# Attention scores: split float32r products of one head, or plain float32 products of two heads in the two row halves of the array

## The chip, the cores and the metric

The kernel runs on one NeuronCore of a Trainium2 chip. Its engines are TensorE (PE in the profile, with its weight loads on a row of their own, PEld), VectorE (DVE), ScalarE (ACT), GpSimd (POOL) and SyncE (SP), which in this kernel issues every DMA. The metric is the device time of one execution in microseconds (us), and lower is better. All inputs lie in device memory when the time begins.

## The reference, cut to what matters

The inputs are q, k, v of 4 batches x 12 heads x 448 tokens x 64 features. Attention with normalised queries and keys is followed by two feed-forward blocks on the 1792 x 768 features.

```python
def rmsnorm(x, g):
    return x / np.sqrt(np.mean(x * x, axis=-1, keepdims=True) + 1e-06) * g
q_n, k_n = rmsnorm(q, g_q), rmsnorm(k, g_k)
scores = q_n @ k_n.T / sqrt(64)                     # per head: 448 x 448
attn = exp(scores - max(scores)); attn = attn / (sum(attn) + 1e-09)
x = attn @ v                                        # heads side by side: 1792 x 768
h = x @ w_in;  x = max(0.01 * h, h) @ w_out         # 768 -> 2048 -> 768
out = ((x @ w1) * (x @ w2)) @ w3 @ w_last           # 768 -> 1024 -> 1024 -> 768
```

## The kernel before, in words

There are 48 heads, taken one by one in slots `s = 0..47`. The 448 query rows of a head are four chunks of 112. In the slot of a head, `scores(s, c)` (L272) makes for each chunk a 112 x 448 tile of scores in PSUM, VectorE scales it, takes the row minimum of the negated scores and writes it to SBUF (`p<-ps`, L289), and ScalarE makes the exponential with its row sum (`p<-p`, L298). One slot later `p_transpose` (L320) turns the four 112 x 448 tiles of a head on TensorE (`pt`, L327, 16 transposes a head), and the results go to SBUF by turns on VectorE and ScalarE (`pth`). Two slots after its scores, every second head, `values` (L349) multiplies the transposed tiles of a pair of heads with v: plain float32 products, 64 columns wide, the two heads in the two column halves of the array, by turns, into one bank (`po`, L121). The helper `together` (L113) keeps these matmuls next to each other.

The products of the feed-forward part, and of the scores, are split: a float32 operand x is rounded to float32r (`xh`), the rest x - xh is a second one (`xl`), and products of the parts are summed in PSUM. For the scores of a head the keys' two parts stand on top of each other in the 128 rows (`ks`: kh in rows 0 to 63, kl in rows 64 to 127), and the queries are there twice (`qt` is loaded into both halves): one matmul with `qh` (L285) and one with `ql` (L286) give all four partial products. `qh` is a copy on ScalarE, `ql` a subtraction on GpSimd (`prep`, L215). The keys of a pair are loaded (`kt_sb`, L255), scaled with the norms on VectorE (L260), rounded on ScalarE (`kh`, L262), subtracted on VectorE (L264), and four DMAs put the parts into `ks` (L268, L269), since the halves of a tile sit in other rows there.

The feed-forward work is one stream of matmul groups (`ps_mm`, L527; three matmuls for each 128 x 128 weight block: wh with xh, wh with xl, wl with xh). `fill` (L1011) puts it between the steps of attention in even shares: first the product of w3 and w_last (`pw`, slots 5 to 17), then the first two batches. Weights arrive as 64-bit words and pass through GpSimd, ScalarE and VectorE before use (`w`, `raw`, `wh`, `wl`; L431 to L488). A planner that simulates the program sets the order of the instructions on each engine, by the priorities in `PRIORITY`; on the chip each engine, SP included, keeps that order. When attention is done (about 800 us), the last two batches run without it (`ps_a`, `ps_b`, `ps_c`, `ps_o`).

```python
ps_sc = right(name="ps_sc", bufs=2, space=PSUM)                                  # L89
nc.tensor.matmul(ps, h["qh"][:, q], h["ks"], start=True, stop=False)             # L285
nc.tensor.matmul(ps, h["ql"][:, q], h["ks"], start=False, stop=True)             # L286
```

Of the kernel before, what the change touches and what calls it, by code (L numbers as in the profile page):

```python
# [8 lines left out]
F32 = mybir.dt.float32  # L9
# [29 lines left out]
MAX_GROUP = 8  # L39
TOGETHER = 2000  # L40
# [8 lines left out]
def attention_then_moe(  # L49
# [39 lines left out]
    ps_sc = right(name="ps_sc", bufs=2, space=PSUM)  # L89
# [97 lines left out]
    def load(i):  # L187
        if i >= NH:
            return
        h = heads[i]  # L190
        b, j = divmod(i, H)
        if i < 2:
            h["k"] = io.tile([CP, NCH, D], F32, tag="rb", name="k_sb", bufs=2)
            nc.sync.dma_start(h["k"], qk[b, j, :, 1])
        h["qt"] = io.tile([P, S], F32, tag="qt", name="qt_sb")
        nc.sync.dma_start(h["qt"][0:D], qt[b, j])
        dma = nc.sync.dma_start(h["qt"][D:P], qt[b, j])
        if i == 2:
            start["ins"] = dma

    def load_v(i):

        if i % 2 or i >= NH:
            return
        b, j = divmod(i, H)
        x = io.tile([CP, 2, NCH, D], F32, tag="v", name="v_sb", bufs=3)
# [17 lines left out]
    def first_keys(i):  # L224

        h = heads[i]
        kn = att.tile([CP, NCH, 2, D], F32, tag="qh", name="kn", bufs=2)
        for e in range(2):
            nc.gpsimd.tensor_tensor(
                kn[:, :, e], h["k"], h["rk"].unsqueeze(2).to_broadcast([CP, NCH, D]), op=ALU.mult  # L230
            )
# [7 lines left out]
        if i == 0:  # L239
            pair = att.tile([P, 2, S], F32R, tag="ks", name="ks", bufs=2)  # L240
            for e in range(2):
                heads[e]["ks"] = pair[:, e]
        ks = h["ks"].rearrange("q (p c) -> q p c", c=NCH)
        pk = pk[:, :S].rearrange("q (c p) -> q p c", c=NCH)
        start["keys"] = nc.scalar.activation(ks, pk, AF.Copy, scale=gqk)
        nc.vector.scalar_tensor_tensor(
            ks[D:P], pk[D:P], gqk[D:P], ks[D:P].bitcast(F32), op0=ALU.mult, op1=ALU.subtract
        )

    def keys(i):  # L250
# [3 lines left out]
        k = io.tile([P, S], F32, tag="kt", name="kt_sb", bufs=1)  # L254
# [10 lines left out]
        pair = att.tile([P, 2, S], F32R, tag="ks", name="ks", bufs=2)  # L265
        for e in range(2):
            rows = slice(e * D, (e + 1) * D)
            nc.sync.dma_start(pair[0:D, e].bitcast(F32), kh[rows].bitcast(F32))  # L268
            nc.sync.dma_start(pair[D:P, e].bitcast(F32), kl[rows].bitcast(F32))  # L269
            heads[i + e]["ks"] = pair[:, e]  # L270

    def scores(i, c):  # L272
        if i >= NH:
            return
        h = heads[i]
        if c == 0:
            h["p"] = [None] * NCH
            if i % 2 == 0:
                sums = small.tile([CP, 2, NCH], F32, tag="sum", name="sum")
                for e in range(2):  # L280
                    heads[i + e]["sum"] = sums[:, e]
                heads[i + 1]["sums"] = sums
# [827 lines left out]
```

## Time and profile before

| what | value |
|---|---|
| time, median of 3 runs | 1256.22 us (1252.75 to 1260.56) |
| the profiled execution, its own time | 1252.88 us |
| its span in the profile | 1251.1 us |
| TensorE busy, mean granted clock | 1151.0 us (92%), 0.962 |
| VectorE / ScalarE / GpSimd busy | 769.4 / 661.4 / 226.5 us |
| moved by DMA | 191.44 MB, 51.0% of the 16 engines' span |

A busy time counts the moments in which an instruction of an engine was under way; matmuls overlap in it, since one begins before the results of the last are written. The granted clock is 1.0 at 2.4 GHz and 0.5 at 1.2 GHz. "A <- B" in a view of waits says that A stood idle until B was done.

### The profile page before, as it was taken

What the parts mean: (1) busy time and instruction counts of PE and PEld (TensorE: products, weight loads), DVE (VectorE), ACT (ScalarE), POOL (GpSimd) and SP (SyncE); (2) the same over time, 40 slices, a digit from 0 to 9 for tenths busy, and PEclk for the clock granted to TensorE, in tenths of its full rate; (3) what the DMA queues carried; (4) which work ended last, traced back from release to release, by engine and by line L of the source; (5) the groups of instructions that cost most, each with busy time, mean ns of one, the idle gap of its engine ahead of it and who ended that gap; (6) DMA issues with size and microseconds to landing.
All of it is one profiled execution on the core that took longest, in us unless ns stands there. A gap on an engine that the chain in (4) does not pass through costs nothing.

```text
span 1251.1 us, 16792 instructions
## 1 busy us (share of the span) xinstructions
PE 1151.0 (92%) x5816; PEld 976.7 (78%) x5816; DVE 769.4 (61%) x1449; ACT 661.4 (53%) x1308; POOL 226.5 (18%) x211
## 2 busy tenths in 40 slices
PE   3659898999888999898999999999999999899998
PEld 1438686876566888686888888899999999799997
DVE  6788776779755466663785355267346465954553
ACT  5766766677656556454765465245442434533431
POOL 4232222334212123213542211100000000000000
PEclk9769999888998999998999999999999999899999
DMA  7777768989889975564464243153212121212212
GB/s 226 195 203 214 215 189 269 292 284 290 251 245 273 240 202 162 151 187 137 148 218 130 79 133 134 53 167 110 81 34 76 35 76 42 73 38 73 63 35 97
DMA packets 105221, 191.44 MB, mean 153 GB/s; under 512 B 22992, under 2 KB 61872, under 8 KB 105136
## 3 DMA queue, kind: packets, MB, share of 16 engines
q1 hardware_dynamic: 105136, 190.37, 51.0%
q8 instruction: 45, 0.74, 0.3%
q14 instruction: 40, 0.33, 0.1%
HBM read 136.74 MB, written 43.03 MB: 144 GB/s over the span
## 4 chain that ended last, share of the span: by engine, by line
PE 54%; DMA 14%; DVE 7%; ACT 4%; issue 3%; SPq 2%; POOL 1%; ACTq 0%; DVEq 0%; POOLq 0%
PE ps_mm L527 19%; PE ps_o L527 13%; PE ps_b L527 9%; PE ps_c L527 5%; DMA w<-w_in 3%; DMA w<-w_out 3%; PE ps_a L527 2%; PE pt L327 2%; PE po L121 2%; DMA ks<-kt_sb 2%; DMA kt_sb<-kt 1%; DMA wh<-kept_first_mlp_h 1%; PE ps L285 1%; DVE raw L460 1%; PE ps L286 1%
## 5 line engine op out<-in xcount | busy, mean ns | idle before, releaser
L213 DVE TENSOR_TENSOR wl<-raw,wh 128x512 fp32r<-128x512 f32 (+1 forms) x136 | 112.6, 831 | 73.0 <-ACT wh L485 37.8
L527 PE MATMUL ps_mm<-xh,wh 128*128 128x448 f32 x384 | 146.6, 383 | 10.6 <-DMA wh<-kept_first_mlp_h 6.9
L327 PE MATMUL pt<-ident,p 112*112 112x112 f32 x768 | 115.3, 276 | 42.2 <-ACT pth L101 21.3
L327 PEld LDWEIGHTS pt<-ident,p 112*112 112x112 f32 x768 | 88.1, 141 | 77.2 <-ACT pth L101 27.6
L289 DVE TENSOR_SCALAR_CACHE_REDUCE p<-ps,rs 112x448 f32<-112x448 f32 x192 | 126.1, 676 | 33.8 <-PE ps L286 20.4
L527 PE MATMUL ps_mm<-xh,wl 128*128 128x448 f32 x384 | 145.5, 379 | 1.5 <-DMA wl<-kept_first_mlp_l 1.5
L298 ACT ACTIVATE p<-p,low 112x448 f32<-112x448 f32 x192 | 127.2, 663 | 36.1 <-DVE p L289 35.7
L527 PE MATMUL ps_mm<-xl,wh 128*128 128x448 f32 x384 | 145.1, 378 | 0.0
L451 ACT ACTIVATE w<-w 128x768 uint32<-128x768 uint32 (+1 forms) x80 | 63.7, 797 | 109.3 <-DMA w<-w_in 36.2
L456 DVE SCALAR_TENSOR_TENSOR raw<-w,raw 128x768 uint32<-128x768 uint32 (+1 forms) x80 | 71.4, 892 | 79.9 <-ACT w L454 79.6
L449 POOL TENSOR_SCALAR raw<-w 128x768 f32<-128x768 f32 (+1 forms) x80 | 70.0, 875 | 265.8 <-DVE wl L213 99.5
L527 PE MATMUL ps_mm<-gh,wh 128*128 128x448 f32 x288 | 106.7, 372 | 2.7 <-DMA wh<-kept_first_mlp_h 1.3
L527 PE MATMUL ps_mm<-gh,wl 128*128 128x448 f32 x288 | 105.7, 369 | 0.0
L527 PE MATMUL ps_mm<-gl,wh 128*128 128x448 f32 x288 | 105.4, 367 | 0.0
L527 PE MATMUL ps_o<-gl,wh 128*128 128x448 f32 x288 | 104.7, 365 | 0.0
L527 PE MATMUL ps_o<-gh,wl 128*128 128x448 f32 x288 | 102.5, 365 | 0.0
L527 PE MATMUL ps_o<-gh,wh 128*128 128x448 f32 x288 | 99.4, 366 | 0.8 <-DVE s L940 0.8
L285 PE MATMUL ps<-ks,qh 128*112 128x448 f32 x192 | 80.2, 422 | 16.4 <-DMA ks<-kt_sb 6.7
L527 PEld LDWEIGHTS ps_mm<-xh,wh 128*128 128x128 f32 x384 | 75.1, 196 | 19.9 <-DMA wh<-kept_first_mlp_h 7.4
L213 POOL TENSOR_TENSOR gl<-y,gh 128x448 fp32r<-128x448 f32 x48 | 58.9, 1229 | 161.6 <-ACT gh L101 154.9
L527 PEld LDWEIGHTS ps_mm<-xh,wl 128*128 128x128 f32 x384 | 75.0, 195 | 10.5 <-issue 2.1
L213 POOL TENSOR_TENSOR ql<-qt_sb,qh 128x448 fp32r<-128x448 f32 x48 | 61.1, 1273 | 114.2 <-ACT qh L101 71.0
(129 smaller groups left out, 2556.1 us busy)
## 6 DMA issues: line engine op xcount, KB each, us to landing
w<-w_in SPq DMA_DIRECT2D x16, 768.0 KB, 7.4
w<-w_out SPq DMA_DIRECT2D x24, 512.0 KB, 5.2
w<-w SPq DMA_DIRECT2D x16, 768.0 KB, 4.9
qk_sb<-qk SPq DMA_DIRECT2D x48, 224.0 KB, 4.9
qt_sb<-qt SPq DMA_DIRECT2D x96, 112.0 KB, 4.0
w<-w3t SPq DMA_DIRECT2D x16, 512.0 KB, 4.6
w<-w_last SPq DMA_DIRECT2D x8, 768.0 KB, 6.2
kept_first_mlp<-raw SPq DMA_DIRECT2D x16, 384.0 KB, 4.0
```

The lines of the kernel that those rows point to most:

```text
L121: one = nc.tensor.matmul(out, a, x, start=begin, stop=end)
L213: e.tensor_tensor(out, x, y.bitcast(F32), op=ALU.subtract)
L285: nc.tensor.matmul(ps, h["qh"][:, q], h["ks"], start=True, stop=False)
L286: nc.tensor.matmul(ps, h["ql"][:, q], h["ks"], start=False, stop=True)
L289: nc.vector.tensor_scalar(p, ps, h["scale"][:, c : c + 1], None, op0=ALU.mult, op1=ALU.min, accum_out=low,)
L298: exps[i] = nc.scalar.activation(p, p, AF.Exp, bias=low, scale=-1.0, accum_out=h["sum"][:, c : c + 1])
L327: nc.tensor.transpose(pt[:, c * CP : (c + 1) * CP], h["p"][c][:, kc * CP : (kc + 1) * CP], ident[:CP, :CP],)
L449: nc.gpsimd.tensor_scalar(out, h, 0.0, 1.0, op0=ALU.mult, op1=ALU.mult)
L451: nc.scalar.activation(low, low, AF.Copy, scale=2.0**-29)
L456: nc.vector.scalar_tensor_tensor(top, high, 3, top, op0=ALU.logical_shift_left, op1=ALU.bitwise_or)
L460: nc.vector.tensor_tensor(top, top, low, op=ALU.add)
L527: nc.tensor.matmul(ps[:, :n], a, x, start=begin, stop=end, skip_group_check=on)
```

## The change

The scores become plain float32 products: the keys of a pair stay as they are after scaling (`kt_sb`, rows 0 to 63 of one head, 64 to 127 of the other), the queries of a pair are loaded once into one tile in the same layout, and a step makes the scores of one chunk for both heads with two matmuls of 64 rows each, one in each half of the array's rows, into the two banks of one PSUM tile. `prep`, the rounding and subtraction of the keys and the four `ks` DMAs are gone. There is one PSUM tile of two banks in place of two tiles of one; `kt` and `qt` have three buffers (one and two before), `p` has twelve in place of seven. Transposes come two slots after the scores and `values` three, since the scores of a pair take two slots, two chunks of both heads in each.

```diff
+PBUFS = 12
...
-    ps_sc = right(name="ps_sc", bufs=2, space=PSUM)
+    ps_sc = right(name="ps_sc", bufs=1, space=PSUM)
...
     def load(i):
-        if i >= NH:
+        if i % 2 or i >= NH:
             return
...
-        h["qt"] = io.tile([P, S], F32, tag="qt", name="qt_sb")
-        nc.sync.dma_start(h["qt"][0:D], qt[b, j])
-        dma = nc.sync.dma_start(h["qt"][D:P], qt[b, j])
+        h["qt"] = io.tile([P, S], F32, tag="qt", name="qt_sb", bufs=3)
+        dma = nc.sync.dma_start(h["qt"], qt[b, j : j + 2].rearrange("h d s -> (h d) s"))
...
-    def prep(i):
-        if i >= NH:
-            return
-        h = heads[i]
-        h["qh"] = att.tile([P, S], F32R, tag="qh", name="qh", bufs=2)
-        copy("A", h["qh"], h["qt"])
-        h["ql"] = att.tile([P, S], F32R, tag="ql", name="ql", bufs=2)
-        subtract("P", h["ql"], h["qt"], h["qh"])
...
     def keys(i):
...
-        k = io.tile([P, S], F32, tag="kt", name="kt_sb", bufs=1)
+        k = io.tile([P, S], F32, tag="kt", name="kt_sb", bufs=3)
...
         nc.vector.scalar_tensor_tensor(k, k, gqk, rk, op0=ALU.mult, op1=ALU.mult)
-        kh = att.tile([P, S], F32R, tag="kh", name="kh", bufs=1)
-        copy("A", kh, k)
-        kl = k.bitcast(F32R)
-        subtract("V", kl, k, kh)
-        pair = att.tile([P, 2, S], F32R, tag="ks", name="ks", bufs=2)
-        for e in range(2):
-            rows = slice(e * D, (e + 1) * D)
-            nc.sync.dma_start(pair[0:D, e].bitcast(F32), kh[rows].bitcast(F32))
-            nc.sync.dma_start(pair[D:P, e].bitcast(F32), kl[rows].bitcast(F32))
-            heads[i + e]["ks"] = pair[:, e]
+        heads[i]["k"] = k
 
     def scores(i, c):
...
-        ps = ps_sc.tile([P, 512], F32, tag="sc", name="ps")[:CP, :S]
         q = slice(c * CP, (c + 1) * CP)
-        nc.tensor.matmul(ps, h["qh"][:, q], h["ks"], start=True, stop=False)
-        nc.tensor.matmul(ps, h["ql"][:, q], h["ks"], start=False, stop=True)
-        p = h["p"][c] = att.tile([CP, S], F32, tag="p", name="p", bufs=7)
...
+        ps = ps_sc.tile([P, 2, 512], F32, tag="sc", name="ps")[:CP, :, :S]
+        one = pair[0]
+        together((ps[:, e], one["qt"][mine(e), q], one["k"][mine(e)], True, True) for e in (1, 0))
+        for e, h in enumerate(pair):
+            p = h["p"][c] = att.tile([CP, S], F32, tag="p", name="p", bufs=PBUFS)
...
     def attention_steps():
 
-        for s in range(NH + 2):
-            ranked(values, s - 2)
+        for s in range(NH + 4):
+            ranked(values, s - 3)
             yield s
             for kc in range(NCH):
-                ranked(p_transpose, s - 1, kc)
+                ranked(p_transpose, s - 2, kc)
                 yield s
-            for c in range(NCH):
-                ranked(scores, s, c)
-                if c == NCH - 1:
-                    ranked(normalise, s)
-                yield s
+            if s < NH:
+                for c in range(2):
+                    ranked(scores, s - s % 2, s % 2 * 2 + c)
+                    if c == 1:
+                        ranked(normalise, s)
+                    yield s
+                    yield s
             ranked(keys, s + KEYS_AHEAD)
-            load_v(s)
-            ranked(prep, s + 2)
+            load_v(s - 1)
             ranked(load, s + 3)
...
-        load(1)
         nc.vector.tensor_tensor(gqk, gg[:, 0:1], gg[:, 1:2], op=ALU.mult)
-        prep(0)
-        first_keys(0)
-        first_keys(1)
-        prep(1)
+        first_keys()
...
-    n = PB * H + 1
+    n = PB * H + 2
```

The order on TensorE in the last quarter of attention, before: chunks of one head, each a `qh` and a `ql` product, between transposes (`pt`) and feed-forward matmuls (`ps_mm`).

```order
L527 MATMUL ps_mm<-gh,wl 128x448
L327 MATMUL pt<-ident,p 112x112 x4
L285 MATMUL ps<-ks,qh 112x448
L286 MATMUL ps<-ks,ql 112x448
L527 MATMUL ps_mm<-gh,wh 128x448
L285 MATMUL ps<-ks,qh 112x448
L286 MATMUL ps<-ks,ql 112x448
L527 MATMUL ps_mm<-gl,wh 128x448
```

The same engine and quarter now; L122 is the matmul inside `together`, and one row stands for the two heads.

```order
L507 MATMUL ps_mm<-gl,wh 128x448
L306 MATMUL pt<-ident,p 112x112 x4
L122 MATMUL ps<-kt_sb,qt_sb 112x448 x2
L306 MATMUL pt<-ident,p 112x112 x4
L507 MATMUL ps_mm<-gh,wl 128x448
```

Four rows of scores have become one row of two matmuls, and it stands between transposes or feed-forward matmuls; some 20 other matmuls lie between it and the next one.

The order on SP near the start, before, between the third load of w_last and the first of w3 (`w_...` are weight tiles, `qk_sb` the rows for the norms, `rk` the keys' norms):

```order
L431 DMA w_858<-w_last 128x1536
L196 DMA qt_sb<-qt 64x448
L146 DMA qk_sb<-qk 112x512
L197 DMA qt_sb<-qt 64x448
L268 DMA ks<-kh 64x448
L146 DMA qk_sb<-qk 112x512
L431 DMA w_914<-w_last 128x1536
L268 DMA ks<-kh 64x448
L269 DMA ks<-kt_sb 64x448 x2
L196 DMA qt_sb<-qt 64x448
L197 DMA qt_sb<-qt 64x448
L255 DMA kt_sb<-kt 128x448
```

SP at the same place now, from the third load of w_last on:

```order
L411 DMA w_690<-w_last 128x1536
L248 DMA rk_sb<-rk_154 64x448 x2
L147 DMA qk_sb<-qk 112x512 x2
L411 DMA w_748<-w_last 128x1536
L147 DMA qk_sb<-qk 112x512 x2
L411 DMA w_788<-w3t 128x1024
L147 DMA qk_sb<-qk 112x512
L411 DMA w_802<-w_last 128x1536
L147 DMA qk_sb<-qk 112x512
L198 DMA qt_sb<-qt 128x448
L244 DMA kt_sb<-kt 128x448
```

The `ks` DMAs and three of four `qt` DMAs of a pair are gone from between the weight loads: from the first to the eighth load of w_last there were 47 DMAs before and there are 30 now.

## Rows read from the trace of the kernel before

**Rows 1.** Busy times by stretch: PE, PEld, DVE, ACT, POOL, granted clock, DMA share, GB/s.

```profile
0.00:100.00 100.00, 55.40 (x224) 38.09 (x225) 77.92 (x166) 65.65 (x127) 32.42 (x34) 0.78 0.75 208
100.00:190.00 90.00, 84.27 (x490) 71.04 (x489) 68.14 (x147) 63.15 (x138) 21.89 (x23) 0.98 0.73 205
190.00:440.00 250.00, 220.41 (x1152) 173.39 (x1151) 168.37 (x354) 162.93 (x358) 68.95 (x62) 0.94 0.91 268
440.00:594.00 154.00, 142.89 (x730) 118.64 (x729) 89.76 (x166) 77.99 (x158) 40.82 (x39) 0.98 0.55 167
594.00:802.00 208.00, 207.39 (x1103) 176.34 (x1103) 115.72 (x205) 116.68 (x225) 57.82 (x50) 1.00 0.42 132
802.00:1251.00 449.00, 440.69 (x2129) 399.20 (x2123) 249.52 (x413) 174.99 (x306) 4.62 (x4) 0.99 0.23 71
```

**Rows 2.** What TensorE waited for up to 594 us: total us, times, longest.

```profile
PE pt L327 <- ACT pth L101: 21.3, 15, 4.5
PE pt L327 <- DVE pth L103: 15.6, 11, 4.3
...
PE ps L285 <- DMA ks<-kt_sb: 6.7, 2, 4.1
```

**Rows 3.** Timeline of PE around the values products of one pair: start, length.

```profile
444.18 0.37 PE L527 MATMUL ps_mm<-gh,wl 128*128 128x448 f32 x1
...
444.79 0.37 PE L527 MATMUL ps_mm<-gh,wl 128*128 128x448 f32 x1
445.08 3.23 PE L121 MATMUL po<-pth,v_sb 112*64 112x448 f32 x16
448.24 0.47 PE L527 MATMUL ps_mm<-gh,wh 128*128 128x448 f32 x1
448.55 0.36 PE L527 MATMUL ps_mm<-gl,wh 128*128 128x448 f32 x1
```

**Rows 4.** Timeline of PE, 444.9 to 445.4 us: the first records of the same products.

```profile
445.08 0.60 PE L121 MATMUL po<-pth,v_sb 112*64 112x448 f32 x2
```

**Rows 5.** Timeline of PE's weight loads inside the same products.

```profile
445.51 0.14 PEld L121 LDWEIGHTS po<-pth,v_sb 112*64 112x64 f32 x2 [0.23 <-issue]
...
446.64 0.14 PEld L121 LDWEIGHTS po<-pth,v_sb 112*64 112x64 f32 x2 [0.23 <-issue]
```

**Rows 6.** Groups by line and form: two kinds of weight load; busy us, mean ns.

```profile
L286 PEld LDWEIGHTS ps<-ks,ql 128*112 128x112 f32 x192 | 35.8, 187 | 3.0 <-POOL ql L213 0.4
...
L121 PEld LDWEIGHTS po<-pth,v_sb 112*64 112x64 f32 x384 | 26.0, 141 | 41.2 <-issue 38.5 <-ACT w L454 0.6 <-DVE raw L456 0.5
```

**Rows 7.** Line 285 by stretch: PE busy (count), PEld, clock, DMA share, GB/s.

```profile
0.00:100.00 100.00, 12.06 (x24) 5.09 (x24) 0.78 0.75 208
100.00:190.00 90.00, 10.98 (x28) 4.96 (x28) 0.98 0.73 205
190.00:440.00 250.00, 31.05 (x76) 13.49 (x75) 0.94 0.91 268
440.00:594.00 154.00, 10.65 (x26) 4.55 (x26) 0.98 0.55 167
594.00:802.00 208.00, 15.47 (x39) 6.84 (x39) 1.00 0.42 132
```

**Rows 8.** DMA issues on the page: count, KB each, median us to landing.

```profile
qt_sb<-qt SPq DMA_DIRECT2D x96, 112.0 KB, 4.0
```

**Rows 9.** Line 269 on SP: issue time ns min/median/max.

```profile
L269 SPq DMA_DIRECT2D ks<-kt_sb x46: 461/588/792, 31.4 to 690.3; - x46
```

**Rows 10.** What SP waited for up to 594 us, two of the longest.

```profile
SPq L196 <- POOL ql L213: 31.6, 14, 9.6
...
SPq L255 <- DMA ks<-kt_sb: 26.0, 14, 4.0
```

**Rows 11.** Line 431 on SP up to 100 us: the loads of w_last.

```profile
L431 SPq DMA_DIRECT2D w<-w_last x8: 353/418/583, 12.4 to 68.0; - x8
```

**Rows 12.** Groups by line and form: the scores' way out of PSUM.

```profile
L289 DVE TENSOR_SCALAR_CACHE_REDUCE p<-ps,rs 112x448 f32<-112x448 f32 x192 | 126.1, 676 | 33.8 <-PE ps L286 20.4 <-PE pt L327 13.4
```

More of the change, by code (lines that the diff above doesn't have):

```diff
@@ L191, in load @@
         b, j = divmod(i, H)
-        if i < 2:
-            h["k"] = io.tile([CP, NCH, D], F32, tag="rb", name="k_sb", bufs=2)
-            nc.sync.dma_start(h["k"], qk[b, j, :, 1])
-        h["qt"] = io.tile([P, S], F32, tag="qt", name="qt_sb")
-        nc.sync.dma_start(h["qt"][0:D], qt[b, j])
-        dma = nc.sync.dma_start(h["qt"][D:P], qt[b, j])
+        if i == 0:
+            h["k"] = io.tile([CP, NCH, 2, D], F32, tag="rb", name="k_sb", bufs=2)
+            for e in range(2):
+                nc.sync.dma_start(h["k"][:, :, e], qk[b, e, :, 1])
+        h["qt"] = io.tile([P, S], F32, tag="qt", name="qt_sb", bufs=3)
+        dma = nc.sync.dma_start(h["qt"], qt[b, j : j + 2].rearrange("h d s -> (h d) s"))
         if i == 2:
@@ L201, in load_v @@
     def load_v(i):
-        if i % 2 or i >= NH:
+        if i % 2 or not 0 <= i < NH:
             return
         b, j = divmod(i, H)
-        x = io.tile([CP, 2, NCH, D], F32, tag="v", name="v_sb", bufs=3)
+        x = io.tile([CP, 2, NCH, D], F32, tag="v", name="v_sb", bufs=2)
         nc.sync.dma_start(x, v[b, j : j + 2].rearrange("h p n d -> p h n d"))
@@ L238, in first_keys @@
             )
-        if i == 0:
-            pair = att.tile([P, 2, S], F32R, tag="ks", name="ks", bufs=2)
-            for e in range(2):
-                heads[e]["ks"] = pair[:, e]
-        ks = h["ks"].rearrange("q (p c) -> q p c", c=NCH)
+        h["k"] = io.tile([P, S], F32, tag="kt", name="k_n", bufs=3)
+        k = h["k"].rearrange("q (p c) -> q p c", c=NCH)
         pk = pk[:, :S].rearrange("q (c p) -> q p c", c=NCH)
[L245 to L248, printed above, removed]
+        start["keys"] = nc.scalar.activation(k, pk, AF.Copy, scale=gqk)
     def keys(i):
@@ L272, in scores @@
     def scores(i, c):
-        if i >= NH:
-            return
-        h = heads[i]
+        pair = heads[i : i + 2]
         if c == 0:
[L277 to L282, printed above, removed]
-        ps = ps_sc.tile([P, 512], F32, tag="sc", name="ps")[:CP, :S]
-        q = slice(c * CP, (c + 1) * CP)
@@ L298, in scores @@
-        exps[i] = nc.scalar.activation(
-            p, p, AF.Exp, bias=low, scale=-1.0, accum_out=h["sum"][:, c : c + 1]
-        )
+            sums = small.tile([CP, 2, NCH], F32, tag="sum", name="sum")
+            for e, h in enumerate(pair):
+                h["p"] = [None] * NCH
+                h["sum"] = sums[:, e]
+            pair[1]["sums"] = sums
+        q = slice(c * CP, (c + 1) * CP)
+        ps = ps_sc.tile([P, 2, 512], F32, tag="sc", name="ps")[:CP, :, :S]
+        one = pair[0]
@@ new lines, in scores @@
+        together((ps[:, e], one["qt"][mine(e), q], one["k"][mine(e)], True, True) for e in (1, 0))
+        for e, h in enumerate(pair):
+            p = h["p"][c] = att.tile([CP, S], F32, tag="p", name="p", bufs=PBUFS)
+            low = small.tile([CP, 1], F32, tag="low", name="low")
+            nc.vector.tensor_scalar(
+                p,
+                ps[:, e],
+                h["scale"][:, c : c + 1],
+                None,
+                op0=ALU.mult,
+                op1=ALU.min,
+                accum_out=low,
+            )
+            exps[i + c // 2] = nc.scalar.activation(
+                p, p, AF.Exp, bias=low, scale=-1.0, accum_out=h["sum"][:, c : c + 1]
+            )
```

23 lines of the change are left out of this document (7 added, 16 removed).

## The prediction

> **What bounds the kernel now.** I read the busy times by stretch first [rows 1], because one number for the whole span mixes different limits. From 594 us on TensorE has no idle time while attention lasts (207.4 of 208 us), and little after it: there only TensorE's own work counts. Before 594 us it is idle for 44.6, 5.7, 29.6 and 11.1 us in the four stretches, 91 us together, a part of it before the first scores. What it waits for there is mostly the emptying of PSUM tiles with transposes (36.9 us on ScalarE and VectorE, [rows 2]), and these two engines are busy 58 to 78% (VectorE) and 51 to 70% (ScalarE) of the four stretches, so no engine of the five is the limit by its sum. Two shared resources are close to full: the DMA engines from 190 to 440 us (a share of 0.91, [rows 1]), and the queue of SP, which has to place every DMA in order, about half a microsecond each [rows 9], and which stands still behind a DMA whose buffer is not free [rows 10]. So the kernel before 594 us is held by transfers that come late, directly or through engines that wait for them in order; after it, by TensorE.
>
> **The change on TensorE.** I call the scores of one chunk for a pair of heads a pair-step; there are 24 x 4 = 96. Before, it is four float32r matmuls. In a dense run such matmuls start 0.203 us apart (444.18 to 444.79 us is three of them, [rows 3]), so a pair-step costs 0.81 us. After, it is two plain float32 matmuls, one in each half of the rows. The trace has no product in row halves. The nearest row is the values product, two heads in the column halves: eight float32 matmuls of 448 columns for two heads are 16 records [rows 3], so each is two; the first records of the two heads run together (two in 0.60 us, [rows 4]); and three steps take 446.64 - 445.51 = 1.13 us [rows 5], so a step of both heads takes 0.376 us. Two steps are 0.75 us, by itself 0.06 less than before. But the values product also pays for entering and leaving: it starts 0.29 instead of 0.203 us after the matmul ahead (+0.09), its first step takes 0.43 (+0.05), after its last step, due at 445.51 + 7 x 0.376 = 448.14, the next matmul begins at 448.24 (+0.10), and the one behind that 0.31 later (+0.10) [rows 3, 5]. That is 0.34 us, for 64 columns of weights; the scores have 112, whose load is 0.187 against 0.141 us [rows 6], so I take 0.39. A pair-step then costs 0.75 + 0.39 = 1.14 us, 0.33 more than before, and the order on TensorE shows that almost each stands alone, so each pays. 96 x 0.33 = 32 us more work for TensorE. The ends: nothing for entering and leaving gives 96 x -0.06 = -6 us; no overlap of the two halves gives 4 x 0.376 + 0.39 = 1.89 us and 96 x 1.08 = +104 us. I take 1.14, since the values product is the same kind of instruction in the same kind of half.
>
> The Trainium skill has a rule against this change: TensorEngine Tiling, section Key Properties, says that a change of the tiling mode drains TensorE. The trace agrees for column halves (the 0.34 us above); by a reading in which halves of rows do not count as another mode the sum would be the -6 us end.
>
> By stretch the 192 qh products [rows 7] put 12, 14, 38, 13 and 19.5 pair-steps into the five stretches, so the 32 us are 4, 4.6, 12.5, 4.3 and 6.4 us. The last is on the path in full.
>
> **What it takes away elsewhere.** Per pair: two rounding copies and a copy of the keys on ScalarE, two subtractions on GpSimd and one on VectorE, seven DMAs of eleven (four `ks`, three `qt`). None of these engines is the limit by its sum, so their work I cost at nothing where it stands; what counts is when transfers come. DMAs: 92 `ks` (46 of line 269 [rows 9] and as many of line 268) and 72 of 96 `qt` [rows 8] go, 164 of 0.5 to 0.6 us each, some 90 us of SP's time; the waits in front of `qt` (31.6 us up to 594 us, for the subtraction that frees the buffer) and of `kt` (26.0 us, for the `ks` DMAs) go too [rows 10]. Of the bytes, 92 x 112 KB and half of 96 x 112 KB, 16 of 191 MB, go. New on SP is the wait of a `kt` load for the scores of three pairs ago; what is queued behind it is weight loads, but those scores are done a slot before, so I cost it at nothing. The lag of one more slot moves the values of the last pair later; feed-forward matmuls of the first two batches still follow them in the order, as before, and hide it.
>
> *0 to 100 us.* SP must place 47 DMAs from the first to the eighth load of w_last, and takes 55.6 us for them [rows 11]; now there are 30. At the same pace that is 35 us, 20 us sooner. VectorE, which must convert those weights, is busy 78% of the stretch [rows 1], so I take half: -10 us. The first pair's and the second pair's scores also come sooner, without the keys' way through `ks` (6.7 us of waits, [rows 2]); this is inside the 10 us.
> *100 to 190 us.* TensorE is busy 94%; 4.6 us more work against 5.7 us of idle time: I take 0.
> *190 to 440 us.* 250 us with 220.4 us of TensorE work, now 233. DMA bytes of nine and a half pairs, 0.69 MB each at the stretch's 268 GB/s, are 24 us of DMA time less, and SP loses 66 of its issues. The floor is 233 us if every wait went; I take 240, -10 us.
> *440 to 594 us.* 142.9 us become 147; SP's waits go, weight conversion stays late: 152 of 154, -2 us.
> *594 to 802 us.* +6 us. *After.* 0.
>
> Sum: -10 + 0 - 10 - 2 + 6 = -16 us, against the profiled execution's 1252.9: 1237 us. That execution is 3 us under the median of the three runs, so for a median I say **1240 us**. Put in other words: 32 us more on TensorE and 48 of 91 us of idle time gone.
>
> **The rivals.**
> *The row halves do not run together* (slower). Place: each pair-step. Price: 1.89 us, +104 us of TensorE work; idle time can pay for some 60 of it (two thirds of the 91), so 1297 us. The forecast turns into a loss where a pair-step costs more than 0.81 + 48/96 = 1.31 us. For it: no row here shows row halves. Against it: the column halves overlap. A milder form is that matmuls start strictly in program order, so that the first record of the second head waits for the second record of the first: 3 x 0.376 + 0.39 = 1.52 us, +68 us, less half of the idle time, 45, 1276 us. The Trainium skill has this as a rule (TensorE: Matmul & The Clock Gate, Part 3, What overlaps and what doesn't: matmuls start and end in strict program order); the first two records of the values product, which begin within one 0.60 us piece, don't bear the delay out. Together 0.09.
> *The emptying becomes the new wait* (slower). Two tiles of scores now come to VectorE at once, 0.68 us each [rows 12], and a transposed tile queued behind them waits 0.68 us longer; TensorE waits for such tiles most already. If half of the 96 second tiles do that, +33 us eat most of the 48: 1270 us. For it: the waits of [rows 2]. Against it: the transposes stand well apart in the order, and VectorE and ScalarE lose work. 0.09.
> *The relief is hidden*: weight conversion on three engines paces the first 594 us whatever SP does, and only absorption pays for the new work: within 1% of before, about 1255 us. For it: DMA share 0.55 and still 11 us of idle time from 440 us on. 0.15.
> *The start gains all of its 20 us and the middle reaches its floor*: 1252.9 - 20 - 17 - 4 + 6 + 3, or the switch costs nothing: 1221 us. 0.17.
>
> **How the numbers follow.** Forecast 0.50, its own range 1226 to 1254. About 1% (12.6 us) is what a measurement of this kernel can tell from no change, so faster means under 1243.6: seven tenths of the forecast and the last rival, 0.35 + 0.17 = 0.52; within 1%: three tenths of the forecast and the hidden relief, 0.30; slower: the first two rivals, 0.18. Range: down to 1210 for the last rival's spread, up to 1280 for the milder form of the first and for the second; left out are the separate halves and the tails.
>
> **What would show it.** In the profile after: score matmuls in pairs of two records that begin within some 10 ns, 0.376 us apart, and a feed-forward matmul about 0.2 us late behind them; the first feed-forward or weight-product matmul earlier; DMA share from 190 to 440 us near 0.86; TensorE idle before 594 us down to some 45 us; the end of attention near 786 us. The forecast is wrong if a pair-step takes over 1.31 us, or if TensorE's waits for transposed tiles grow.

## The result, and the profile after

The changed kernel takes 1264.66 us (median of 19 runs, 1254.62 to 1270.79), the kernel before 1254.77 us beside it (19 runs). The ratio is 1.007 (95% interval 1.005 to 1.009): 9 to 10 us slower, inside the 1% that I named as no change, but on the other side of the forecast of 1240 us. The profiled execution has a span of 1262.0 us.

The windows of the kernel after, by the stretches of [rows 1] (the last one ends with its span):

```profile
0.00:100.00 100.00, 58.21 (x239) 34.30 (x240) 76.02 (x170) 66.11 (x126) 20.31 (x26) 0.90 0.70 208
100.00:190.00 90.00, 82.34 (x453) 60.57 (x452) 59.60 (x134) 53.66 (x116) 12.18 (x15) 0.96 0.58 167
190.00:440.00 250.00, 223.58 (x1140) 151.44 (x1140) 151.06 (x334) 146.39 (x324) 44.21 (x43) 0.97 0.77 238
440.00:594.00 154.00, 148.51 (x751) 112.87 (x752) 89.86 (x175) 77.44 (x160) 30.57 (x32) 0.99 0.45 140
594.00:802.00 208.00, 203.70 (x1052) 161.97 (x1053) 108.90 (x196) 104.59 (x202) 45.85 (x42) 0.99 0.39 126
802.00:1262.00 460.00, 451.81 (x2186) 408.55 (x2184) 251.90 (x416) 178.88 (x312) 5.82 (x5) 0.99 0.22 70
```

The DMA share from 190 to 440 us fell from 0.91 to 0.77, further than forecast, and every other engine has less to do. Still TensorE's idle time before 594 us is 41.8 + 7.7 + 26.4 + 5.5 = 81 us, where [rows 1] give 91 and I forecast 45. The last values product begins at 810.1 us, 10.6 later than before, and that lateness stays to the end.

What TensorE of the kernel after waits for up to 594 us (us, times, longest), beside [rows 2]:

```profile
PE ps L122 <- DVE p L268: 34.1, 16, 5.9
PE pt L306 <- ACT pth L102: 18.6, 19, 2.9
...
PE pt L306 <- DVE pth L104: 3.4, 4, 1.6
```

The kernel before has this row for its two score tiles:

```profile
PE ps L285 <- DVE p L289: 4.7, 7, 1.1
```

The waits for transposed tiles fell from 36.9 to 22.0 us, and those for the keys' DMAs are gone. In their place stands the first row: score products that wait until VectorE has emptied the one score tile. Before, that wait was 4.7 us. By stretch it is uneven: 28.7 of the 34.1 us lie in the first 100 us.

The timeline of the kernel after shows both the price of a pair-step and one such wait (start, length, engine, line):

```profile
48.31 1.01 PE L122 MATMUL ps<-kt_sb,qt_sb 64*112 64x448 f32 x4
...
49.71 0.96 DVE L436 SCALAR_TENSOR_TENSOR raw<-w,raw 128x768 uint32<-128x768 uint32 x1 [0.68 <-ACT w L434]
...
51.28 0.95 DVE L214 TENSOR_TENSOR lastl<-raw,lasth 128x768 fp32r<-128x768 f32 x1
52.14 0.95 DVE L440 CUSTOM_DVE_ANT_0 raw<-w,raw 128x1536 uint16<-128x1536 uint16 x1
...
53.11 0.68 DVE L268 TENSOR_SCALAR_CACHE_REDUCE p<-ps,rs 112x448 f32<-112x448 f32 x1
...
53.72 0.69 DVE L268 TENSOR_SCALAR_CACHE_REDUCE p<-ps,rs 112x448 f32<-112x448 f32 x1
...
54.46 1.84 PE L122 MATMUL ps<-kt_sb,qt_sb 64*112 64x448 f32 x4 [3.88 <-DVE p L268]
...
607.69 0.36 PE L507 MATMUL ps_mm<-gl,wh 128*128 128x448 f32 x1
608.05 1.01 PE L122 MATMUL ps<-kt_sb,qt_sb 64*112 64x448 f32 x4
608.99 0.47 PE L507 MATMUL ps_mm<-gh,wl 128*128 128x448 f32 x1
609.30 0.36 PE L507 MATMUL ps_mm<-gh,wh 128*128 128x448 f32 x1
```

The price: the four records of a pair-step start within 0.47 us, in pairs 6 to 7 ns apart in the trace, so the row halves do run together. From 608.05 to 608.99 is 0.94 us; the matmul behind comes 0.31 later in place of 0.203; the entry takes 0.30 by the median over the trace (0.36 in this one). That makes 0.94 + 0.31 + 0.30 - 2 x 0.203 = 1.14 us, the forecast's figure [rows 3 to 5].
The wait: the products of 48.31 are done at some 49.3 us. VectorE has three steps of weight conversion (L436, L214, L440) ahead of the emptying in its queue, and starts it at 53.11. TensorE's next score product, which needs the same tile, and everything queued behind it stand for 3.88 us.

Last, the loads of w_last on SP, as [rows 11]:

```profile
L411 SPq DMA_DIRECT2D w<-w_last x8: 327/346/456, 7.1 to 53.1; - x8
```

The eighth is placed at 53.1 in place of 68.0 us, 15 us sooner. From the first to the eighth SP takes 46.0 us for 30 DMAs, where I forecast 35: the pace of the kernel before did not hold. And TensorE has finished no more work by 190 us than before (82.34 + 58.21 against 84.27 + 55.40 us of busy time, of which some 8 us, 25 pair-steps by 0.33, are the longer products).

### The profile page after: what moved, and what is told of

The parts are those of the page before. It is cut to its first block, busy times and chain, and to the rows that moved or that the text cites. A ratio compares the mean times of both kernels' runs of the same rounds, so it can differ in the third digit from the quotient of the medians.

```text
span 1262.0 us, 16277 instructions
## 1 busy us (share of the span) xinstructions
PE 1168.2 (93%) x5812; PEld 929.7 (74%) x5812; DVE 737.3 (58%) x1424; ACT 627.1 (50%) x1236; POOL 158.9 (13%) x161
## 4 chain that ended last, share of the span: by engine, by line
PE 51%; DMA 22%; DVE 11%; ACT 9%; issue 3%; SPq 1%; POOL 1%; ACTq 0%; DVEq 0%; POOLq 0%
PE ps_mm L507 17%; PE ps_o L507 12%; PE ps_b L507 9%; DMA w<-w_out 6%; PE ps_c L507 5%; DMA w<-w 3%; DMA w<-w3t 3%; DVE raw L436 2%; DMA w<-w_in 2%; PE ps_a L507 2%; DMA rk<-rs 2%; PE ps L122 2%; PE po L122 2%; ACT p L277 2%; PE pt L306 2%
## 5 line engine op out<-in xcount | busy, mean ns | idle before, releaser
L214 DVE TENSOR_TENSOR wl<-raw,wh 128x512 fp32r<-128x512 f32 (+1 forms) x136 | 109.2, 806 | 105.9 <-ACT wh L465 70.2
L268 DVE TENSOR_SCALAR_CACHE_REDUCE p<-ps,rs 112x448 f32<-112x448 f32 x192 | 123.2, 680 | 43.2 <-PE ps L122 40.5
L507 PE MATMUL ps_mm<-xh,wh 128*128 128x448 f32 x384 | 143.5, 376 | 4.7 <-DMA wh<-kept_first_mlp_h 3.5
L306 PEld LDWEIGHTS pt<-ident,p 112*112 112x112 f32 x768 | 83.2, 138 | 87.2 <-ACT pth L102 31.3
L306 PE MATMUL pt<-ident,p 112*112 112x112 f32 x768 | 111.5, 273 | 27.1 <-ACT pth L102 21.2
L436 DVE SCALAR_TENSOR_TENSOR raw<-w,raw 128x768 uint32<-128x768 uint32 (+1 forms) x80 | 68.4, 855 | 91.5 <-ACT w L434 91.1
L122 PE MATMUL ps<-kt_sb,qt_sb 64*112 64x448 f32 x368 | 98.9, 616 | 19.3 <-DVE p L268 19.2
L429 POOL TENSOR_SCALAR raw<-w 128x768 f32<-128x768 f32 (+1 forms) x80 | 66.3, 829 | 373.1 <-DVE wl L214 230.1
L507 PE MATMUL ps_mm<-gl,wh 128*128 128x448 f32 x288 | 108.0, 376 | 0.7 <-POOL gl L214 0.7
L214 POOL TENSOR_TENSOR gl<-y,gh 128x448 fp32r<-128x448 f32 x48 | 58.8, 1227 | 199.7 <-ACT gh L102 180.2
L507 PEld LDWEIGHTS ps_mm<-xl,wh 128*128 128x128 f32 x384 | 73.1, 190 | 10.8 <-issue 4.7
```

The costliest lines, as they stand in the source:

```text
L122: one = nc.tensor.matmul(out, a, x, start=begin, stop=end)
L214: e.tensor_tensor(out, x, y.bitcast(F32), op=ALU.subtract)
L268: nc.vector.tensor_scalar(p, ps[:, e], h["scale"][:, c : c + 1], None, op0=ALU.mult, op1=ALU.min, accum_out=low,)
L306: nc.tensor.transpose(pt[:, c * CP : (c + 1) * CP], h["p"][c][:, kc * CP : (kc + 1) * CP], ident[:CP, :CP],)
L429: nc.gpsimd.tensor_scalar(out, h, 0.0, 1.0, op0=ALU.mult, op1=ALU.mult)
L436: nc.vector.scalar_tensor_tensor(top, high, 3, top, op0=ALU.logical_shift_left, op1=ALU.bitwise_or)
```

## The experiments

Every run was timed in five rounds beside the kernel before. The ratio is to the kernel before, and differences of time below go by the medians or by these ratios, which can differ by some 3 us; busy and idle are TensorE's in the profiled execution (idle is the span less the page's busy time); the last column is the score products' wait for VectorE up to 594 us. "Rows" means products over all 128 rows, "halves" two heads at once in the row halves; a count by a time, as 4 x 0.198, is records by the time of one. Where a kernel leaves out a part of the scores or uses shortened numbers, its expectation says so; such a kernel only serves to time its parts.

| kernel | pair-step, us | us | ratio (95%) | busy | idle | wait |
|---|---|---|---|---|---|---|
| before | rows, 0.81 | 1255 to 1258 | 1 | 1151.0 | 100.1 | 4.7 |
| after | halves, 1.14 | 1264.7 | 1.007 (1.005, 1.009) | 1168.2 | 93.8 | 34.1 |
| x1 | halves, 224 keys | 1217.8 | 0.967 (0.964, 0.970) | 1131.8 | 82.2 | 11.2 |
| x2 | halves, doubled | 1349.4 | 1.071 (1.068, 1.075) | 1236.4 | 112.7 | 38.1 |
| x3 | as after | 1314.4 | 1.044 (1.041, 1.047) | 1185.1 | 128.7 | 24.4 |
| x4 | as after | 1265.7 | 1.005 (1.003, 1.007) | 1165.3 | 98.9 | 36.2 |
| x5 | rows, 4 x 0.198 | 1214.8 | 0.966 (0.963, 0.968) | 1136.1 | 76.9 | 13.9 |
| x6 | as after | 1298.5 | 1.031 (1.027, 1.034) | 1183.9 | 115.0 | 32.5 |
| x7 | as after | 1323.4 | 1.051 (1.047, 1.054) | 1188.5 | 135.8 | 12.4 |
| x8 | as after, few in twos | 1330.8 | 1.057 (1.054, 1.061) | 1189.6 | 138.1 | 12.2 |
| x9 | rows, 6 x 0.198 | 1248.5 | 0.994 (0.991, 0.996) | 1168.9 | 80.4 | 15.8 |
| x10 | as x5 | 1246.4 | 0.992 (0.990, 0.995) | 1147.5 | 99.5 | 19.3 |
| x11 | as x5 | 1229.1 | 0.979 (0.977, 0.982) | 1138.0 | 89.3 | 11.1 |
| x12 | halves, 3 float32r | 1260.9 | 1.004 (1.002, 1.006) | 1160.0 | 106.7 | 21.3 |
| x13 | halves, 3 x 0.198 | 1246.1 | 0.992 (0.989, 0.995) | 1147.8 | 93.5 | 21.8 |
| x14 | as after | 1272.7 | 1.013 (1.010, 1.016) | 1170.4 | 100.7 | 30.4 |
| x15 | as after | 1264.0 | 1.006 (1.004, 1.009) | 1166.9 | 99.5 | 39.4 |
| x16 | as after | 1265.2 | 1.008 (1.005, 1.011) | 1168.7 | 93.7 | 31.9 |
| x17 | as after | 1265.9 | 1.006 (1.003, 1.008) | 1168.3 | 95.9 | 31.8 |
| x18 | rows, 4 x 0.376 | 1283.1 | 1.020 (1.017, 1.023) | 1206.4 | 76.9 | 15.0 |

### Less and more TensorE work: x1, x2

x1 multiplies only the first 224 keys, and VectorE reads them twice. x2 does each product twice.

```diff
 x1
-        together((ps[:, e], one["qt"][mine(e), q], one["k"][mine(e)], True, True) for e in (1, 0))
+        together(
+            (ps[:, e, : S // 2], one["qt"][mine(e), q], one["k"][mine(e), : S // 2], True, True)
...
+                ps[:, e, : S // 2].unsqueeze(1).to_broadcast([CP, 2, S // 2]),
 x2
+        together((ps[:, e], one["qt"][mine(e), q], one["k"][mine(e)], True, True) for e in (1, 0, 1, 0))
```

> The changed kernel with the score products of only the first 224 keys of each head, which are then read twice, so that VectorE and ScalarE do the same work; the other half of the scores is left out. A pair-step should cost TensorE 0.376 + 0.37 = 0.75 instead of 1.13 us, 36 us less in all. If TensorE's price of the pair-steps is what made the change slower, most of it shows: 25 to 36 us less than the changed kernel (1229 to 1240 us). If the early part is paced by late transfers and by the single score tile, only the part from 594 us on shows in full and the rest is swallowed: 8 to 14 us less.

> The changed kernel with every score product done twice in a row into the same banks: 2 x 0.376 us more per pair-step, 72 us more TensorE work, nothing else. If TensorE paces the kernel, 60 to 72 us more (1325 to 1337 us); if idle time before 594 us can swallow work, as the prediction took for granted, 25 to 45 us more.

36 us less busy time gained some 49 us on the kernel after; 68 us more cost 82. Both lie beyond the larger of the two ranges that I gave. TensorE's idle time swallows none of a longer pair-step; it even grows with it (82.2, 93.8 and 112.7 us). A reading that fits, not shown, is that the engines TensorE waits for themselves follow its products.

x2 also settles how entering and leaving is paid. Its four products of a step stand together:

```profile
685.31 1.76 PE L122 MATMUL ps<-kt_sb,qt_sb 64*112 64x448 f32 x8
687.00 0.59 PE L306 MATMUL pt<-ident,p 112*112 112x112 f32 x4
```

From start to start that is 1.69 us, where two products take 0.94: 0.75 us more, which is two steps of 0.376 and no second entry. The price is paid once a visit, as the prediction had it.

### The removed transfers, first try, and VectorE's order: x3, x4

x3 puts the 164 removed DMAs back into one spare tile that nobody reads. x4 gives VectorE's emptying the highest priority.

```diff
 x3, in keys; three more of the kind in load
+        spare = att.tile([P, 2, S], F32, tag="ks", name="ks", bufs=1)
+        for e in range(2):
+            rows = slice(e * D, (e + 1) * D)
+            nc.sync.dma_start(spare[0:D, e], k[rows])
+            nc.sync.dma_start(spare[D:P, e], k[rows])
 x4
+            with tc.high_priority(TOGETHER):
+                nc.vector.tensor_scalar(
```

> The changed kernel with the removed transfers put back into a spare tile that nobody reads: four copies of 112 KB of the scaled keys per pair and three loads of 112 KB of queries per pair, 164 DMAs, 18 MB. If fewer transfers are what paid for part of the new TensorE work, as the prediction says, it is 12 to 25 us slower than the changed kernel. If the freed DMA and queue time was hidden anyway, within 4 us of it.

> The changed kernel with VectorE's reading of the score tile put ahead of other work in VectorE's order. If the waits of score products for the single tile (34 us before 594 us) cost time, 10 to 25 us less than the changed kernel, and these waits fall under 15 us. If they only stand where TensorE would have waited for something else, within 5 us, and idle time moves to other waits.

x3 costs some 46 us, more than expected, but it is not clean: with one spare tile SP stands behind each spare DMA until the one before has landed (56.0 us of such waits up to 594 us for the loads of queries, 20.6 for the copies of keys). x4 changes nothing, and does not test its expectation: the order of the instructions on every engine came out the same as in the kernel after.

### The relief without the longer products, and the score tile: x5 to x8

```diff
 x5
+        def short(x):
+            return x.bitcast(mybir.dt.bfloat16).rearrange("p (s t) -> p s t", t=2)[:, :, 1]
+        quick = short(one["qt"]), short(one["k"])
+        together((ps[:, e], quick[0][:, q], quick[1][:], n == 0, n == 1) for e in (1, 0) for n in range(2))
 x6: ps_mm bufs 3 -> 2, ps_pt bufs 2 -> 1
 x7: x6 and ps_sc bufs 1 -> 2
 x8: x7, and both chunks of a slot in one
...
+                (tiles[n][:, e], one["qt"][mine(e), (c + n) * CP : (c + n + 1) * CP], one["k"][mine(e)], True, True)
+                for n in range(2)
+                for e in (1, 0)
```

> The changed kernel with its two-bank score tile, its halved q loads and without the 164 DMAs, but its products done as four one-pass matmuls over all 128 rows, as many and as long as the kernel before has (16-bit halves of the same words, both heads' rows summed, so the scores are not the reference's). So it is the relief without the dearer pair-step. Theory 1 (the relief is real, and the price of the pair-step, 96 x 0.33 = 32 us, goes to the end in full or more, because TensorE's idle time is not slack): 32 to 43 us under the changed kernel, 20 to 35 us under the kernel before, about 1225 to 1237 us. Theory 2 (something else, the weights' conversion above all, paces the first 594 us, and the relief there is hidden): only what comes after 594 us changes, 0 to 6 us under the kernel before. Theory 3 (waits for the one score tile eat the relief): the waits stay near 34 us and the time is 0 to 15 us under the kernel before.

> The changed kernel with two banks less, one of the feed-forward results' three and one of the transposes' two: only a control for the next two. Slower than the changed kernel by 5 to 40 us, since TensorE waits for emptied transposes already.

> The control before with its two spare banks given to a second score tile. Theory 3 (the single score tile's wait, 34 us in the changed kernel up to 594 us, is on the path): 15 to 30 us under the control, and the wait of score products for VectorE falls below 12 us. Theory 1 (the wait is only the place where TensorE meets VectorE's place in the order; without it TensorE waits for something else): within 8 us of the control.

> The kernel before this one (two score tiles), with the products of two chunks, four matmuls, back to back, so that the row halves are entered and left 48 times and not 96. If entering and leaving is paid once a stretch (0.39 us of the predicted pair-step): 48 x 0.39 = 19 us less TensorE work, and by theory 1 15 to 25 us under it. If the price lies in each product: no change in TensorE's work. Two tiles needed at once may cost back up to 10 us of waits for VectorE.

x5, the first part of the page (busy us, share, records):

```profile
PE 1136.1 (94%) x5812; PEld 954.6 (79%) x5812; DVE 740.3 (61%) x1424; ACT 628.1 (52%) x1236; POOL 164.7 (14%) x161
```

With products as short as before (0.79 against 0.81 us), the rest of the change is worth 42 us: 1257.0 to 1214.8. That is more than any of the three theories said; theory 1 has the right direction, and theory 2 (the relief is hidden) falls. Against the kernel before TensorE is idle 23 us less, and busy 15 us less for nearly the same work, at a mean granted clock of 0.983 where it was 0.962. Against x5 the kernel after has 1168.2 - 1136.1 = 32.1 us more TensorE work, the very 32 of the forecast, and some 51 us more time.

In x7 TensorE waits up to 594 us for these:

```profile
PE pt L306 <- ACT pth L102: 30.3, 25, 5.3
PE pt L306 <- DVE pth L104: 24.3, 15, 7.3
PE ps L122 <- DVE p L268: 12.4, 8, 4.5
```

A second score tile does take the waits for the score tile away (32.5 to 12.4 us), but with one transposed tile they come back there (24.7 to 54.6), and x7 is 25 us slower than its control. Theory 3 is not upheld, nor is it disproved, since the bank had to come from the transposes; x6 shows what two banks fewer cost alone, some 30 us. x8 did not do what it was made for. In most places feed-forward matmuls still stand between the two steps, as here:

```profile
642.23 1.01 PE L122 MATMUL ps<-kt_sb,qt_sb 64*112 64x448 f32 x4
643.17 0.47 PE L514 MATMUL ps_mm<-gh,wl 128*128 128x448 f32 x1
643.56 1.01 PE L122 MATMUL ps<-kt_sb,qt_sb 64*112 64x448 f32 x4
```

Two steps stand together 25 times in x8, and 24 times in x7 without that edit. So its busy time (1189.6 against 1188.5) says nothing on the entries; x2 does.

### Which relief, and which length: x9 to x12

x9 is x5 with six products a pair-step in place of four (`range(3)`). x12 has float32r parts, made once a pair. The core of the others:

```diff
 x10, on x5, in keys and load
+        for e in range(4):
+            nc.sync.dma_start(spare[i // 2, e, :, :S], k[mine(e % 2)])
...
+        with tc.issue_after(dma.ins):
+            for e in range(3 if i else 0):
+                nc.sync.dma_start(spare[i // 2, 4 + e, :, :S], qt[b, j + e % 2])
 x11, on x5, once a pair
+        copy("A", spare[:, 0], h["qt"])
+        copy("A", spare[:, 0], h["qt"])
+        copy("A", spare[:, 0], h["k"])
+        subtract("P", spare[:, 1], h["qt"], h["k"])
+        subtract("P", spare[:, 1], h["qt"], h["k"])
 x12, on after
+            copy("A", hi, x)
+            subtract(eng, lo, x, hi)
...
+            for n, (a, x) in enumerate((("qh", "kh"), ("qh", "kl"), ("ql", "kh")))
```

> The relief kernel of x5 (one-pass products over all 128 rows, scores not the reference's) with six such products a pair-step in place of four: 6 x 0.198 = 1.19 us, which is nearly the changed kernel's pair-step of 1.13 us, but with no row halves, none entered or left, and another order by the planner. Theory 1 (the length of the pair-step on TensorE decides, whatever makes it long): 96 x 0.40 = 38 us more work than x5 and 38 to 60 us more time, 1253 to 1275 us, about the changed kernel's time. Theory 4 (the row halves, or the order that the planner makes for float32 products, cost more than their length says): only the 38 us or less, under 1252 us.

> The relief kernel of x5 with 161 of the 164 removed DMAs put back, each of 64 rows of 1792 B as before, but from the q input or the keys' tile into DRAM that nobody reads, so that none waits for a buffer and no product waits for them. Theory 1 (SP's issues and the bytes are the relief): 25 to 45 us over x5, 1240 to 1260 us, back to the kernel before. Rival (the rounding and subtracting that ScalarE, VectorE and GpSimd lost is the relief): within 10 us of x5.

> The relief kernel of x5 with three copies of 128x448 on ScalarE and two subtractions on GpSimd put back per pair, at the place where the kernel before had them, into a spare tile that nobody reads; no DMA more. Theory 1 (costed at nothing, as in the prediction): within 10 us of x5. Rival: 20 to 40 us over x5, since ScalarE stands in the way of the transposed tiles.

> The changed kernel with its one load of q and k for two heads and its row halves, but both split into two float32r parts once a pair (two copies on ScalarE, a subtraction on GpSimd and one on VectorE), and the scores as three float32r products a head in the row halves; the q and k tiles have one buffer, keys are made two slots later, and the transposed tiles have eight buffers and the probabilities eleven. Pair-step 3 x 0.203 + 0.39 = 1.00 us against 1.14: 13 us less TensorE work. Theory 1 (1.6 us of time for each us of it): 15 to 21 us under the changed kernel, less up to 10 us for the split and up to 15 us for the buffers: 1245 to 1270 us, and with no cost for those two below the kernel before. If entering and leaving the halves costs more with float32r products: above 1270 us.

x10 from 190 to 440 us:

```profile
190.00:440.00 250.00, 224.53 (x1216) 174.89 (x1216) 165.48 (x360) 156.83 (x345) 47.02 (x45) 0.96 0.95 287
```

The DMAs alone cost 32 us, and bring the DMA share back to 0.95 (0.79 in x5): theory 1 of x10 (SP's issues and the bytes are the relief) holds. The copies and subtractions cost 14 us, outside the 10 that I allowed: they are not free. Together 46, where the relief is 42.
x9: 32.8 us more busy time and 33.7 us more time than x5: length alone costs what it is long. x9 has the kernel after's TensorE busy time to within 1 us, and is 17 us faster (ratios 1.007 and 0.994): theory 4 (the halves, or the order made for them, cost more than their length). So by relief and length alone the change would be a gain of 8 us. x12, whose pair-step takes 0.99 us where I expected 1.00, is busy 8 us less than the kernel after in place of 13, and no faster than the kernel before; it also has fewer buffers.

### Where the other 17 us come from: x13 to x18

x13 is x9 with three products a head in the halves (`quick[0][mine(e), q], quick[1][mine(e)]`). x14, x15: scores with priority 400, 800. x16: `CONVERT_PRIORITY = 300`. x18: `one["qt"][:, q], one["k"]`, all rows, in float32. x17:

```diff
+    def behind(t):
+        return tc.issue_after(start["read"].ins) if t >= 24 else ExitStack()
...
+            start["read"] = nc.vector.tensor_scalar(
...
+            with behind(t):
                 nc.vector.scalar_tensor_tensor(
...
+            with behind(t):
                 nc.vector.tensor_tensor(top, top, low, op=ALU.add)
...
+            with behind(t):
                 subtract("V", flat[1], x, flat[0])
```

> The kernel of x9 (six one-pass products a pair-step, scores not the reference's) with its six products in the two halves of the rows, three a head, as the changed kernel places its two; the planner makes nearly the same order as for x9. By steps of 0.198 us with two heads at once and the 0.39 us for entering and leaving, a pair-step is 0.98 us, 0.21 less than x9's. Theory L (row halves cost what their pair-step is long and no more; the 17 us left over are the order): 96 x 0.21 = 20 us under x9, 1225 to 1235 us. Theory H (row halves cost the extra 17 us, by what TensorE does around them): 1240 to 1250 us.

> The changed kernel, its instructions all the same, but scores with a priority of 400 in place of 600, under the transposes'. Theory L (the order makes the 17 us): another order gives another time, by 8 us or more, and one of this and the next two comes near 1248 us. Theory H: all three within 6 us of the changed kernel.

> The changed kernel, its instructions all the same, but scores with a priority of 800, over the transposes'. Expected as for the kernel with 400.

> The changed kernel, its instructions all the same, but the conversion of weights with a priority of 300 in place of 100, over the values' 200. Expected as for the kernel with scores at 400; if what feeds the weights paces the first 594 us, this one is the fastest of the three.

> The changed kernel, its instructions all the same, but from the 25th weight tile on VectorE's three steps of a tile's conversion are queued behind the emptying of the last score tile that the code wrote before them. Theory B (the 17 us are the emptying's place in VectorE's queue): emptying begins within 1.2 us of the products' end from 190 to 440 us, and 8 to 18 us are gained on the changed kernel, 1247 to 1257 us. Rival (the place in the queue is only a sign): within 6 us of the changed kernel, or slower by up to 20 us, since weights then come later.

> The changed kernel with its two float32 products over all 128 rows instead of the halves (both heads' rows summed, so the scores are not the reference's): they can't run at once, so a pair-step is four records of 0.376 us, 1.50 us against 1.13, with nothing entered or left. TensorE's work grows by 96 x 0.37 = 36 us. Theory L and H (the length on the chip decides): 1295 to 1310 us. Theory B (the planner's order, which counts on this length anyway, decides): within 15 us of the changed kernel, 1262 to 1280 us, with fewer waits of score products for VectorE.

What TensorE waits for in x18, up to 594 us:

```profile
PE ps L122 <- DVE p L268: 15.0, 8, 4.6
PE pt L306 <- ACT pth L102: 13.0, 13, 3.1
```

The same in x13:

```profile
PE ps L122 <- DVE p L272: 21.8, 9, 5.3
PE pt L310 <- ACT pth L102: 19.8, 12, 3.6
...
PE pt L310 <- DVE pth L104: 7.8, 4, 3.0
```

The kernels with products over all rows are idle for nearly the same time, whatever their length: x5, x9 and x18 are busy 1136.1, 1168.9 and 1206.4 us and idle 76.9, 80.4 and 76.9. The kernel after has 38.2 us of busy time less than x18, and 16.9 us more idle time; x13 has 21.1 us less than x9 and 13.1 us more idle time, and the medians differ by 2 us. x1, in halves and about as short as x5, has 5 us more idle time than x5 and is 3 us slower. So theory L fails as I had put it (x13 came out at 1246 in place of 1225 to 1235). Theory H gave x13's time (1240 to 1250), but a fixed 17 us for the halves does not fit x1. Theory B of x18 (the planner's order decides: within 15 us of the kernel after) missed by 3 us, and so did the other side (1295 to 1310). What holds in all three comparisons: kernels in halves have more idle time on TensorE, and for the kernel after and x13 that is nearly half or more of the busy time saved.

Not all three isolate the halves, since the planner makes a new order when the products change. Before the second pair's values product TensorE has 99 feed-forward and weight-product matmuls in the kernel after, 48 in x18, and 24 in both x9 and x13. The orders of x9 and x13, and of x5 and x1, are nearly the same; those of the kernel after and x18 or x9 are not. x14 to x16 are the kernel after's instructions in other orders: two lie within 1 us of it and x14 8 us above, as theory L had allowed, but none came near 1248 us. That speaks against the order as the reason, for the orders tried.

Where the 17 us stand is less plain than the row for the score tile suggests. Up to 594 us that wait is 34.1 us in the kernel after, 15.8 in x9 and 15.0 in x18. But 28.7 of the 34.1 lie in the first 100 us. In that stretch the kernel after waits, and then x9:

```profile
PE ps L122 <- DVE p L268: 28.7, 8, 5.9
```
```profile
PE ps L122 <- DVE p L272: 13.6, 6, 4.0
PE pt L310 <- ACT pth L102: 12.1, 5, 4.5
```

The busy times of x9 in that stretch and from 190 to 594 us, and those of the kernel after for the second:

```profile
0.00:100.00 100.00, 58.99 (x262) 40.57 (x263) 73.98 (x162) 61.85 (x113) 20.13 (x26) 0.85 0.72 201
190.00:594.00 404.00, 385.32 (x2093) 303.69 (x2092) 258.56 (x557) 234.04 (x506) 79.27 (x79) 0.99 0.66 205
```
```profile
190.00:594.00 404.00, 372.09 (x1889) 264.31 (x1888) 240.91 (x509) 223.83 (x484) 74.78 (x74) 0.97 0.65 201
```

In the first 100 us the kernel after is idle 41.8 us and x9 41.0 (x18 37.3): where the kernel after waits 15 us longer for the score tile, x9 waits some 11 us longer for transposed tiles (12.8 against 1.7). From 190 to 594 us the kernel after is idle 31.9 us and x9 18.7: 13.2 us, about all of the 13.4 by which the idle times of the two traces differ. What the kernel after waits for at PSUM tiles in that stretch, and then x9:

```profile
PE pt L306 <- ACT pth L102: 11.6, 13, 2.9
...
PE ps L122 <- DVE p L268: 3.6, 6, 1.2
PE pt L306 <- DVE pth L104: 2.9, 3, 1.6
```
```profile
PE pt L310 <- ACT pth L102: 5.4, 3, 2.8
...
PE ps L122 <- DVE p L272: 1.7, 1, 1.7
PE pt L310 <- DVE pth L104: 0.9, 1, 0.9
```

The score tile accounts for 2 us of the difference there, transposed tiles for 8. So the waits for the score tile are the largest new row, but they are not shown to be what the 17 us consist of.

Nor is the reason behind them shown. From 190 to 440 us VectorE begins the emptying on average 2.0 us after the products' end in the kernel after (mean over its 38 pair-steps, last score record's end to the first L268), 1.4 in x18, 1.2 in x13, 0.9 in x9. x17 brought that to 1.6, not under the 1.2 that its theory asked for, and gained nothing (31.8 us of waits for the tile were left); its edit begins with the 25th weight tile, which VectorE converts after 170 us, so it left the first 100 us as they were. Weight conversion ahead in the queue, as in the timeline above, is where the wait is seen, not shown to be its cause. Whether a second score tile that costs no other bank would bring the 17 us back stays open: x7 could not tell, since its second tile came at the transposes' cost.

## Why the prediction was wrong

*Right: the pair-step.* 1.14 us forecast, 1.14 in the trace; 32 us of TensorE work forecast, 32.1 of busy time between x5 and the kernel after. Halves do overlap, so the first rival falls in both forms: the trace shows the first records of the two heads 7 ns apart.

*Right in size, wrong in its parts: the relief.* I forecast 48 us of idle time; x5 shows 42 us of time. Put back, the DMAs cost 32 us (x10), and the rounding and subtracting, costed at nothing, 14 (x11). Only 23 us of it are idle time; 15 us are shorter busy time, which goes with a higher granted clock (in the first 100 us 0.95 in x5 against 0.78 before). "The relief is hidden" falls with x5.

*The step that failed* is the term "48 of 91 us of idle time gone". TensorE's idle time before 594 us fell only from 91 to 81 us, and over the span by 6, from 100.1 to 93.8. With short products over all rows 23 us of it go (76.9 in x5), and 17 us are back in the kernel after, with the halves and the order made for them; the sum has no term for that. It also let idle time pay for longer products, as in the 0 from 100 to 190 us; x9 and x18 show that it pays for none. With -42 for the relief and +34 for the length (x9) the change would be at 1248 us; the 17 us more make it 1265.
What the sum left out in the kernel is the score tile: two tiles of one bank became one of two, and I priced what its emptying does to the transposes, but not what it does to the next score product, whose wait went from 4.7 to 34.1 us. How much of the 17 us that wait costs stays open, since in the first 100 us it mostly takes the place of other waits.
The rival "the emptying becomes the new wait" named the engine and the 0.68-us reads. Against the kernel before its place is wrong, since transposed tiles wait less than before, and its sign in the last paragraph ("or if TensorE's waits for transposed tiles grow") did not come; against x9, from 190 to 594 us, they do wait longer.

*By stretch.* 0 to 100 us: the eighth w_last load did come 15 us sooner, yet nothing was left of it at 190 us. 190 to 440: forecast -10; the stretch has 3 us less idle time and 12.5 us more work. 594 to 802: forecast +6; TensorE has 4 us of idle time there that it had not, and the values products slip from 7 us late (the 19th pair, 621.8 to 629.1 us) to 11 (the last).

## What to carry to other kernels

When an engine's work gets shorter by running two things at once, ask what it will wait for instead: here nearly half of the busy time saved against x18 came back as idle time. Give each buffer count that a change lowers a price of its own, at the producer as well as at the consumers behind it. Do not take the row of waits that grew most for the cost: compare the idle time of the same stretch in a kernel without it. Split a change of many parts on the chip before believing its sum: the same relief with short products is a 42-us gain, and the products' length (34 us) and their form with its order (17 us) lost it.

## What the hardware showed that I had not expected

TensorE's idle time is no slack even where it is 8% of the span: from x5 to x9 and on to x18, 32.8 and 37.5 us more busy time cost 33.7 and 34.6 us. Entering the halves takes as long for products of 16 bits as for float32: in x13 the first product starts 0.30 us behind a feed-forward matmul, as in the kernel after (median), and much as the values product did (0.29, [rows 3]). Float32r products run in row halves too (in x12 the two heads' first records start 3 ns apart). One buffer fewer for transposes and one for feed-forward results cost some 30 us (x6).
